# A planned three-layer kernel on one core: the order of the work found anew with other prices for changes of array form, and 49 filler products where there were 60

## The chip, the cores and the metric

The kernel runs on one core of one Trainium2 chip. The metric is the device time of one execution in microseconds (us). Lower is better. TensorE is called PE here, VectorE DVE, ScalarE ACT, GpSimd POOL, and SyncE, which issues the DMAs, SP.

## What is computed

Three layers follow each other on 4 batches of 576 positions, all in float32: an attention of 8 heads over a window of 64 positions, a gated layer that mixes positions, and a top-2 choice among 4 experts, each of which is a causal attention of one head.

```python
# 1: windowed attention, head_dim 64
scores = scale * q @ k^T ; mask = (rel >= 0) & (rel < 64)
x = softmax(where(mask, scores, -1e9)) @ v          # to (B, S, 512)
# 2: gated mixing of positions
h = maximum(x @ w_in, 0) ; u, v = h[..., :512], h[..., 512:]
v_n = (v - mean(v)) / sqrt(var(v) + 1e-6)
v_s = einsum('ts,bsd->btd', w_spatial, v_n) + b_spatial
x = (u * v_s) @ w_out
# 3: top 2 of 4 experts
logits = x @ w_gate ; topk = argpartition(-logits, 2)[..., :2] ; w = softmax(selected logits)
for e in range(4):
    a = softmax(causal(scale * (x @ wq[e]) @ (x @ wk[e])^T))
    out += where(e in topk, w, 0) * (a @ (x @ wv[e]) @ wo[e])
```

## The kernel before, in words

The large products take each float32 operand as a high and a low part and add three products (`mm3`); these are the instructions that stand in the trace as `xh,w`, `xl,w`, `w,xh` and so on. They use the whole array, 128 rows by 128 columns. Other products use parts of it, and their groups stand in the trace with the array in front of the shape:

- form 0: the whole array (`b_v`, `b_u`, `b_mix`, `fold` in the first stage, `c_qk`, `c_v`, `c_vt`, `c_wo` in the second), and the transposes (`p_t`, L647; `tr`, L1329), which have no form of their own before
- form 1: scores of the windowed attention, `s_mm`, 64*64, 24 instructions for one *couple* (two groups of three blocks of 64 queries)
- form 2: products of probabilities and values, `pv` and `c_pv`, 128*64
- form 3: scores of the experts' attention, `three`, 64*128

The order of the instructions on every engine is made by a planner that runs while the kernel is built (class `Planner`, L169 to L306). Each piece of work is a node (`N(...)`) with a price in ns on each engine that may do it, what it depends on, the buffers that it takes, and a priority out of the list `KEY`. The planner keeps a clock. When an engine is free, it takes the ready node with the lowest key whose buffers are free. `SWITCH` is added to the key of a node on PE that would change the array's form, `DRAIN` is the time that it counts for such a change. Where DVE, ACT or POOL may do a node, `DVE_BIAS`, `POOL_BIAS` and `EFT` decide how willingly an engine takes it. What it puts out is a fixed order on each engine with semaphore waits; on the chip nothing is chosen.

There are two planned stages, one after the other. Stage 1 holds 1,130 nodes: loads, preparation of the weights (`prep64` and others, on DVE, ACT and POOL), the windowed attention of all batches (24 couples: `s_mm`, masked scores L629, exponentials L635, normalisation L643, transposes, copies, `pv`), the gated layer of all batches, and the `fold` of `w_out` into the experts' weights. The gated layer of one batch runs beside the windowed attention of the next. Stage 2 is the experts' layer, in which P is normalised at L1317 on DVE or POOL and then transposed. A node of stage 2 comes behind all of stage 1 on its engine.

`heat` makes filler products on the identity matrix: `WARM` = 8 of them in front of everything, and `FILL` = 60 nodes that have the highest key there is, so that the planner takes one where nothing else is ready on PE. All of them must be placed before stage 1 ends. Each is two instructions in the trace (`bank<-ident`).

Of the kernel before, what the change touches and what calls it, by code (L numbers as in the profile page):

```python
# [26 lines left out]
SWITCH = (51316.5562883, 56444.76665)  # L27
A_BIAS = 10098.0
C_BIAS = 162315.0
DVE_BIAS = (924.812225719, 2809.18155958)  # L30
POOL_BIAS = (605.73769693, 3223.06614942)
WARM = 8
FILL = 60
LOADS = (-130000, -120000, -43801, -5807, 14591, 18276, 34028)
EFT = (348.130120865, 591.3127716)
# [6 lines left out]
    1e+09, 1e+09, 1e+09, 1e+09, 1e+09, 1e+09, 1e+09, 1e+09, 1e+09, 1e+09, 1e+09, 1e+09, 1e+09, -433949.337, -310768.212, -410360.675, -53326.873, -46012.043, -29718.587, 29893.476, 36423.798, 130640.442, 48760.892, -102410.634,  # L42
# [132 lines left out]
class Node:  # L175
    __slots__ = ("on", "emit", "prio", "wait", "next", "ready", "alloc", "use", "end", "by", "late", "form", "nth", "sbuf")


class Planner:

    LAT = 200.0, 165.0, 130.0, 75.0, 900.0
    ISSUE, WAY, RATE, FLIGHT = 475.0, 650.0, 360.0, 8

    DRAIN = (0.0, 145.0, 145.0, 92.0), (0.0, -78.0, 0.0, 0.0), (0.0, 0.0, -78.0, 0.0), (0.0, 0.0, 0.0, -92.0)

    CLASH, BEHIND = 1.0, 2200.0

    def __init__(self):
        self.nodes, self.free, self.prio = [], [1500.0, 2000.0, 2900.0, 7600.0, 560.0], 0.0
        self.moved, self.unit = [-1e9] * self.FLIGHT, 0
        self.phase = self.form = self.asked = 0
        self.sbuf = False

    def node(self, on, emit, deps=(), alloc=(), use=(), prio=None, late=None, form=0, sbuf=False):
        n = Node()
        n.form, n.nth, n.sbuf = form, self.asked, sbuf
# [1317 lines left out]
```

## Time and profile before

| | us |
|---|---|
| median of 3 runs | 441.62 |
| the runs | 441.45 to 443.12 |
| the profiled execution | 441.42 |
| its span, first to last instruction | 439.6 |
| PE busy in it | 432.1 |
| DVE, ACT, POOL busy | 288.6, 275.8, 90.0 |

The profile is of one execution. A timeline row is an instruction or a run of like ones: its start, how long it lasts, engine, line, operation, what it writes and reads, the array in use and the shape. Products overlap, so the length of a row holds the end of the pipe too, and the distance between two starts is what a block costs in a row of others. A line can be that of a helper: L416 is `mm`, through which all products go, L440 is `sub`.

### The profile page before, as it was taken

To read this page: it belongs to the slowest core of one execution; us is meant where nothing else is said; L and a number is where in the kernel's file an instruction comes from. 1 tells how busy PE (TensorE), PEld (TensorE's weight loads), DVE (VectorE), ACT (ScalarE), POOL (GpSimd) and SP (SyncE) were. 2 spreads that over 40 slices of the span, in tenths; PEclk is the share of its full clock that TensorE was granted. 3 is DMA by queue.
4 is the path that set the end of the run, shared out by engine and by line. 5 is a ranking of instruction groups with operands and counts; after the bars stand their busy time and mean duration, and the time that the engine had idled before them with its cause. 6 is when DMAs were issued, how large, how long until landed. Compare 5 with 4: busy or idle time off the path is not lost.

```text
span 439.6 us, 10921 instructions
## 1 busy us (share of the span) xinstructions
PE 432.1 (98%) x4058; PEld 390.0 (89%) x4058; DVE 288.6 (66%) x1238; ACT 275.8 (63%) x883; POOL 90.0 (20%) x132
## 2 busy tenths in 40 slices
PE   8999999999999999999999999999999999999997
PEld 7988989998889989998999999999799978987775
DVE  4999998695787583354435444977654956498750
ACT  4899986787785273352433352867576748557873
POOL 4556754121041050001100120120012101110000
PEclk9999999999999999999999999999999999999999
DMA  8995614364145020121001000000020002000114
GB/s 269 339 343 151 238 51 154 96 205 120 38 108 147 1 73 0 49 73 49 1 1 50 0 1 1 0 2 2 1 97 1 1 1 98 1 0 2 49 51 143
DMA packets 31079, 33.11 MB, mean 75 GB/s; under 512 B 1905, under 2 KB 24689, under 8 KB 31026
## 3 DMA queue, kind: packets, MB, share of 16 engines
q1 hardware_dynamic: 31026, 32.41, 23.5%
q8 instruction: 32, 0.52, 0.5%
q14 instruction: 21, 0.17, 0.1%
HBM read 27.68 MB, written 4.72 MB: 74 GB/s over the span
## 4 chain that ended last, share of the span: by engine, by line
PE 84%; DVE 10%; ACT 3%; issue 1%; DMA 1%; POOL 1%; SPq 0%; DVEq 0%; POOLq 0%; ACTq 0%
PE bank L416 75%; PE bank L1329 5%; PE bank L647 4%; DVE p L1307 3%; DVE p L1300 2%; DVE p L1317 1%; ACT p L1313 1%; DMA kt<-in_kT_dram 1%; POOL p L1317 1%; DVE mc L1315 1%; DVE qk L440 0%; DVE mc L1316 0%; ACT pa L635 0%; DVE t2w L440 0%; DVE pa L629 0%
## 5 line engine op out<-in xcount | busy, mean ns | idle before, releaser
L416 PE MATMUL bank<-xh,w 128*128 128x288 f32 x512 | 109.5, 298 | 0.0
L416 PEld LDWEIGHTS bank<-xh,w 128*128 128x128 f32 x512 | 84.1, 188 | 1.4 <-issue 0.3
L416 PE MATMUL bank<-xl,w 128*128 128x288 f32 x256 | 75.5, 295 | 0.0
L416 PE MATMUL bank<-w,xh 128*128 128x512 f32 (+1 forms) x256 | 64.8, 343 | 0.0
L635 ACT ACTIVATE pa<-pa,mx 128x128 f32<-128x128 f32 x144 | 55.8, 393 | 12.7 <-DVE mx L629 12.6
L1313 ACT ACTIVATE p<-p,mc 128x256 f32<-128x256 f32 (+4 forms) x72 | 41.5, 577 | 15.5 <-DVE mc L1307 13.7
L416 PEld LDWEIGHTS bank<-xl,w 128*128 128x128 f32 x256 | 48.1, 188 | 0.4
L416 PEld LDWEIGHTS bank<-w,xh 128*128 128x128 f32 x256 | 43.0, 188 | 5.0 <-DVE mx L651 0.2
L416 PE MATMUL bank<-w,xl 128*128 128x512 f32 (+1 forms) x128 | 43.2, 338 | 0.0
L1317 POOL TENSOR_SCALAR p<-p,mc,fx 128x384 f32<-128x384 f32 (+4 forms) x22 | 14.6, 664 | 133.8 <-DVE mc L1316 66.8
L416 PE MATMUL bank<-wsp_h,vh 128*128 128x288 f32 x128 | 38.9, 304 | 0.0
L416 PE MATMUL bank<-wsp_l,vh 128*128 128x288 f32 x128 | 37.7, 294 | 0.0
L416 PE MATMUL bank<-wsp_h,vl 128*128 128x288 f32 x128 | 37.7, 294 | 0.0
L1307 DVE CUSTOM_DVE_ANT_0 p<-bank,cmask 128x512 f32<-128x512 f32 (+3 forms) x64 | 28.8, 487 | 4.8 <-PE bank L416 2.4
L629 DVE CUSTOM_DVE_ANT_0 pa<-bank,mask 128x128 f32<-128x128 f32 x120 | 28.2, 286 | 4.4 <-PE bank L416 4.3
L853 POOL TENSOR_TENSOR st<-st,nhalf 128x1 f32<-128x1 f32 (+1 forms) x20 | 11.8, 592 | 92.2 <-DVE st L852 56.6
L427 ACT ACTIVATE pg<-bank 128x512 f32<-128x512 f32 (+4 forms) x80 | 29.7, 438 | 0.7 <-PE bank L1329 0.2
L1329 PE MATMUL bank<-ident,p 128*128 128x128 f32 x192 | 27.2, 276 | 1.7 <-DVE p L1317 0.7
L427 ACT ACTIVATE pt<-bank 128x384 f32<-128x384 f32 x41 | 18.4, 486 | 15.8 <-PE bank L647 15.8
L635 ACT ACTIVATION_READ_ACCUMULATOR pa<-pa,mx 128x1 f32 x144 | 27.6, 192 | 0.0
L416 PEld LDWEIGHTS bank<-w,xl 128*128 128x128 f32 x128 | 24.1, 188 | 2.8
L1329 PEld LDWEIGHTS bank<-ident,p 128*128 128x128 f32 x192 | 21.6, 140 | 5.5 <-DVE p L1317 2.6
(193 smaller groups left out, 989.9 us busy)
## 6 DMA issues: line engine op xcount, KB each, us to landing
vt<-in_v_dram SPq DMA_DIRECT2D x12, 512.0 KB, 5.0
qa<-in_qT_dram SPq DMA_DIRECT2D x44, 96.0 KB, 4.4
out_dram<-ot SPq DMA_DIRECT2D x15, 256.0 KB, 2.1
y<-in_w_in_dram SPq DMA_DIRECT2D x7, 512.0 KB, 6.2
kt<-in_kT_dram SPq DMA_DIRECT2D x12, 288.0 KB, 5.3
y<-in_w_outT_dram SPq DMA_DIRECT2D x4, 512.0 KB, 4.2
y<-in_wspT_dram SPq DMA_DIRECT2D x2, 576.0 KB, 4.0
vt<-in_kq_dram SPq DMA_DIRECT2D x2, 384.0 KB, 3.8
```

What stands on the lines that cost most here:

```text
L416: pe.matmul(o, lhsT, rhs, start=start, stop=stop)
L427: act.activation(o, i, AF.Copy)
L629: dve.tensor_tensor_reduce(out=pa[:, j, :], in0=ps[:, j * 128:(j + 1) * 128], in1=mask(j), scale=-0.125, scalar=3.0e38, op0=ALU.add, op1=A ...
L635: act.activation(pa[:, j, :], pa[:, j, :], AF.Exp, bias=mx[:, j, 0:1], scale=-1.0, accum_out=mx[:, j, 1:2])
L647: pe.transpose(ps2[:, j * 128:(j + 1) * 128], pa[:, j, :], ident)
L853: a = N((POOL, 464), lambda e: pool.tensor_tensor(out=st[:m, 9:10], in0=st[:m, 8:9], in1=nhalf[:m], op=ALU.pow), [n1], use=[st])
L1300: dve.tensor_tensor_reduce(out=P[HALF[y], a0:a1], in0=ps[y][HALF[y], :HS], in1=cmask[HALF[y], 0:HS] if i == 0 else tmask[HALF[y]], scale=- ...
L1307: tops = [N((DVE, t_tt(L)), lambda _, ps=ps: dve.tensor_tensor_reduce(out=P[:, cs], in0=ps[:, cs], in1=cmask[:, 512 - L:512], scale=-0.125 ...
L1313: a = N((ACT, 284 + 0.87 * L), lambda e: act.activation(P[:, cs], P[:, cs], AF.Exp, bias=mc[:, 0:1], scale=-1.0, accum_out=mc[:, 2:3]), to ...
L1315: a = N((DVE, 70), lambda e: dve.tensor_scalar(mc[:, 3:4], mc[:, 2:3], 1e-9, None, op0=ALU.add), [a], use=[mc], prio=prio)
L1317: a = N({POOL: 328 + 0.832 * L, DVE: 90 + 0.52 * L}, lambda e: engs[e].tensor_scalar(P[:, cs], P[:, cs], mc[:, 3:4], fx[:, I, ev:ev + 1], ...
L1329: pe.transpose(ps[:, j * m:(j + 1) * m], P[:, c0 + j * 128:c0 + (j + 1) * 128], ident)
```

## The change

All of it is in the planner's input and in its prices. `KEY`, with one number for each node, is another list (2,028 numbers that are not a filler's, and 49 fillers'). The fillers go from 60 to 49. `SWITCH`, which was added once where PE goes between form 0 and any other, is now multiplied by the time of the change, out of a table for every pair of forms, and transposes are a form of their own (4), which costs nothing beside form 0. The prices of nodes on PE no longer hold the changes. The normalisation of P at L1317 is priced at 190 ns and not 90 on DVE, besides its elements. The biases of DVE and POOL change. No instruction's shape, operand or buffer changes.

```diff
-SWITCH = (51316.5562883, 56444.76665)
+SWITCH = (3449.06880151, 1241.9455123)
-DVE_BIAS = (924.812225719, 2809.18155958)
-POOL_BIAS = (605.73769693, 3223.06614942)
+DVE_BIAS = (909.043169196, 5820.53335932)
+POOL_BIAS = (256.434349454, 4103.69459824)
-FILL = 60
+FILL = 49
-EFT = (348.130120865, 591.3127716)
+EFT = (137.341113842, 3173.43987937)
 KEY = (
...
-    DRAIN = (0.0, 145.0, 145.0, 92.0), (0.0, -78.0, 0.0, 0.0), (0.0, 0.0, -78.0, 0.0), (0.0, 0.0, 0.0, -92.0)
+    DRAIN = ((0.0, 138.0, 137.0, 191.0, 0.0),
+             (212.0, 0.0, 158.0, 212.0, 165.0),
+             (204.0, 151.0, 0.0, 204.0, 157.0),
+             (194.0, 141.0, 140.0, 0.0, 147.0),
+             (0.0, 145.0, 144.0, 198.0, 0.0))
...
-                    key = n.prio + (SWITCH[self.phase] if e == PE and (n.form > 0) != (self.form > 0) else 0.0), n.nth
+                    key = n.prio + (SWITCH[self.phase] * self.DRAIN[self.form][n.form] if e == PE else 0.0), n.nth
...
-        S_N[n0] = S_N[n0 + 1] = top = N((PE, 816), s_mm, kn + [Q_N[n0], Q_N[n0 + 1], S_N.get(n0 - 1)], alloc=bank, use=hk, prio=prio,
+        S_N[n0] = S_N[n0 + 1] = top = N((PE, 654), s_mm, kn + [Q_N[n0], Q_N[n0 + 1], S_N.get(n0 - 1)], alloc=bank, use=hk, prio=prio,
...
-            a = N((PE, 327), p_t, [a], alloc=[ps2, pt], use=[pa], prio=prio)
+            a = N((PE, 327), p_t, [a], alloc=[ps2, pt], use=[pa], prio=prio, form=4)
...
-        o = N((PE, 848), pv, done + [PV_N.get(k[:2]) for k in grp] + vn, alloc=[ps3] + new, use=pts + hv, prio=prio,
+        o = N((PE, 699), pv, done + [PV_N.get(k[:2]) for k in grp] + vn, alloc=[ps3] + new, use=pts + hv, prio=prio,
...
-        a = N({POOL: 328 + 0.832 * L, DVE: 90 + 0.52 * L}, lambda e: engs[e].tensor_scalar(
+        a = N({POOL: 328 + 0.832 * L, DVE: 190 + 0.52 * L}, lambda e: engs[e].tensor_scalar(
```

The same is done in stage 2: `three`, `c_pv` and `c_wo` lose what their prices held for a change, and the transposes `tr` get form 4.

## Rows read from the trace of the kernel before

**Rows 1.** Page: busy us by engine; PE's granted clock, 40 slices, tenths.

```profile
PE 432.1 (98%) x4058; PEld 390.0 (89%) x4058; DVE 288.6 (66%) x1238; ACT 275.8 (63%) x883; POOL 90.0 (20%) x132
PEclk9999999999999999999999999999999999999999
```

**Rows 2.** By stage: length, engines' busy us, granted clock, DMA share, GB/s.

```profile
0.00:25.30 25.30, 23.83 (x298) 21.81 (x299) 19.39 (x98) 17.61 (x66) 13.36 (x36) 1.00 0.96 306
25.30:60.00 34.70, 33.70 (x354) 29.12 (x353) 32.09 (x136) 33.80 (x115) 21.58 (x23) 1.00 0.65 215
60.00:256.00 196.00, 196.00 (x1962) 182.72 (x1961) 120.13 (x463) 107.14 (x357) 36.66 (x49) 1.00 0.23 66
258.60:436.30 177.70, 175.98 (x1429) 153.76 (x1427) 115.32 (x544) 114.48 (x339) 18.15 (x25) 1.00 0.07 26
```

**Rows 3.** Timeline, PE, 0 to 30 us: start, us, engine, line, operation, tiles, shape.

```profile
5.18 1.56 PE L416 MATMUL bank<-vt 64*64 64x128 f32 x24
8.65 0.89 PE L416 MATMUL bank<-vt 64*64 64x128 f32 x24
24.39 0.83 PE L416 MATMUL bank<-ident 128*128 128x128 f32 x6
25.31 0.71 PE L416 MATMUL bank<-w,xh 128*128 128x512 f32 x2
```

**Rows 4.** Timeline of DVE, 8 to 34 us.

```profile
23.12 0.56 DVE L643 TENSOR_TENSOR pa<-pa,mx 128x384 f32<-128x384 f32 x1
24.54 0.33 DVE L440 TENSOR_TENSOR xl<-bank,xh 128x192 fp32r<-128x192 f32 x1
```

**Rows 5.** Timeline of PE, 60 to 80 us.

```profile
63.04 0.29 PE L416 MATMUL bank<-xh,w 128*128 128x288 f32 x1
63.26 0.92 PE L416 MATMUL bank<-pt,vt 128*64 128x64 f32 x24
64.11 0.89 PE L416 MATMUL bank<-kt,qa 64*64 64x128 f32 x24
...
65.78 0.89 PE L416 MATMUL bank<-kt,qa 64*64 64x128 f32 x24
66.59 0.40 PE L416 MATMUL bank<-wsp_h,vh 128*128 128x288 f32 x1
66.83 0.30 PE L416 MATMUL bank<-wsp_l,vh 128*128 128x288 f32 x1
...
78.18 1.62 PE L416 MATMUL bank<-pt,vt 128*64 128x64 f32 x48
79.73 0.40 PE L416 MATMUL bank<-wsp_h,vh 128*128 128x288 f32 x1
```

**Rows 6.** Timeline of PE, 255 to 262 us.

```profile
256.02 2.84 PE L416 MATMUL bank<-ident 128*128 128x128 f32 x24
258.62 0.49 PE L416 MATMUL bank<-w,xh 128*128 128x260 f32 x2
```

**Rows 7.** Timeline of POOL, 248 to 266 us.

```profile
254.13 0.81 POOL L440 TENSOR_TENSOR xl<-pa,xh 128x288 fp32r<-128x288 f32 x1 [9.05 <-ACT xh L427]
```

**Rows 8.** Waits of PE's weight loads from 256 us: us, times, longest.

```profile
PEld bank L1329 <- DVE p L1317: 2.6, 7, 0.7
PEld bank L1329 <- POOL p L1317: 1.5, 4, 0.6
```

**Rows 9.** Groups by line and shape: busy us, mean ns, idle before them.

```profile
L1317 DVE TENSOR_SCALAR p<-p,mc,fx 128x384 f32<-128x384 f32 x8 | 3.8, 479 | 0.1
L1317 POOL TENSOR_SCALAR p<-p,mc,fx 128x384 f32<-128x384 f32 x8 | 6.2, 770 | 37.8 <-DVE mc L1316 22.4 <-ACT oh L427 15.4
```

**Rows 10.** Page: groups of masked scores, exponentials and copies of stage 1.

```profile
L629 DVE CUSTOM_DVE_ANT_0 pa<-bank,mask 128x128 f32<-128x128 f32 x120 | 28.2, 286 | 4.4 <-PE bank L416 4.3
L635 ACT ACTIVATE pa<-pa,mx 128x128 f32<-128x128 f32 x144 | 55.8, 393 | 12.7 <-DVE mx L629 12.6
L427 ACT ACTIVATE pt<-bank 128x384 f32<-128x384 f32 x41 | 18.4, 486 | 15.8 <-PE bank L647 15.8
```

More of the change, by code (lines that the diff above doesn't have):

```diff
@@ L41 @@
     1e+09, 1e+09, 1e+09, 1e+09, 1e+09, 1e+09, 1e+09, 1e+09, 1e+09, 1e+09, 1e+09, 1e+09, 1e+09, 1e+09, 1e+09, 1e+09, 1e+09, 1e+09, 1e+09, 1e+09, 1e+09, 1e+09, 1e+09, 1e+09,
-    1e+09, 1e+09, 1e+09, 1e+09, 1e+09, 1e+09, 1e+09, 1e+09, 1e+09, 1e+09, 1e+09, 1e+09, 1e+09, -433949.337, -310768.212, -410360.675, -53326.873, -46012.043, -29718.587, 29893.476, 36423.798, 130640.442, 48760.892, -102410.634,
[85 rows of a table removed]
+    1e+09, 1e+09, -367151.352, -349921.894, -357607.274, -121393.737, -140326.89, -100931.392, -99031.673, -73271.671, -58056.097, -50110.204, -166770.302, -122982.601, -358667.696, -358903.944, -385197.421, -358202.174, -359433.768, -163314.009, -121448.521, -110265.225, -229129.906, -275481.363,
[84 rows of a table added]
 )
@@ L1253, in scores @@
                 ps = [r_sc.new(), r_sc.new()]
-                a = N((PE, 92 + 3 * t_mm(HS)), lambda _, ps=ps, i=i: three(
+                a = N((PE, 3 * t_mm(HS)), lambda _, ps=ps, i=i: three(
                     [p[:, :HS] for p in ps], (S - 64, S - 128), i * HS, (i + 1) * HS),
@@ L1269, in go @@
                 c += w
-        a = N((PE, 92 + sum(3 * t_mm(128 * I + 128) for I in tiles)), go, deps, alloc=ps + pp + gets, use=[qk], prio=prio, form=3)
+        a = N((PE, sum(3 * t_mm(128 * I + 128) for I in tiles)), go, deps, alloc=ps + pp + gets, use=[qk], prio=prio, form=3)
         started(a)
@@ L1336, in unit @@
         f, an = a, PG_N[key][:1]
-        a = N((PE, nj * 109), tr, [f] + an, alloc=[ps], use=[P], prio=prio)
+        a = N((PE, nj * 109), tr, [f] + an, alloc=[ps], use=[P], prio=prio, form=4)
         a = N(on_copy(nj * m, 1), tc_, [a], use=[ps, pg], prio=prio)
@@ L1344, in unit @@
             a = N((PE, 109), lambda _: pe.transpose(pt[:64, :128], P[:, 512:576], ident), [f] + PG_N[key][:1], alloc=[pt],
-                  use=[P], prio=prio)
+                  use=[P], prio=prio, form=4)
             a = N(on_copy(128), lambda e_: copy(e_, pg[HALF[hb], 3, :, 64 * hb:64 * hb + 64],
@@ L1372, in c_pv @@
         cs = slice(i0, i0 + 256)
-        o = N((PE, 800 if grp == 0 else 2200), go, PG_N[b, pr, grp] + V2_N[b] + (VT_N[b] if grp else []) + ([] if new else O_N[b, pr][:1]),
+        o = N((PE, 651 if grp == 0 else 2056), go, PG_N[b, pr, grp] + V2_N[b] + (VT_N[b] if grp else []) + ([] if new else O_N[b, pr][:1]),
               alloc=[ps] + new, use=[pg, v2] + ([vt] if grp else []), prio=prio, form=2)
@@ L1417, in c_wo @@
             return
-        a = N((PE, 78 + 6 * t_mm(512)), lambda e: mm3(ps.t, [
+        a = N((PE, 6 * t_mm(512)), lambda e: mm3(ps.t, [
             ((part(0, pr), part(1, pr)), (view(wh.t)[:, pr, :], view(wl.t)[:, pr, :])) for pr in range(2)]),
```

169 rows, old and new, of the table KEY are left out of this document.

## The prediction, made before the change was run

> **What bounds the kernel now.** I read the page's busy times first. TensorE (PE) is busy for 98% of the span at a granted clock of full speed in every slice [rows 1], so time can only go where PE does something that the result does not need, or stands. The table by stage says where that is [rows 2]: from 25.3 us on, PE is busy in practically all of every stage, while VectorE (DVE) and ScalarE (ACT) have slack from 60 us on (DVE 120 of 196 us). Busy is not the same as useful, so the third view is PE's timeline, read by the distance from one start to the next. It shows four things.
>
> The head. Until 25.31 us PE waits for its first 128x512 products, and the 60 filler products stand in the gaps: 48 of them there, each a pair of instructions on `ident` (fp32 goes as two), the last three at 24.39 us [rows 3]. What ends the head is the attention chain and not PE: DVE's last `xl` at 24.54 us comes 0.4 us ahead of that first product [rows 4].
>
> The changes of array form. A block of 24 `pv` products (array 128*64) takes 0.85 us to the next start where a block of another form follows it, and two of them in a row take 1.55 us (78.18 to 79.73) [rows 5]: 0.70 for the one that is followed by its like, so the change costs 0.15. A visit from 128x288 products and back, at 63.26 to 66.59 us, has 0.22 us instead of 0.13 in front of its first product, and 0.24 instead of 0.13 behind its first full product [rows 5]. In between lie four blocks, `pv`, `s_mm`, `pv`, `s_mm`, with 0.85, 1.67 (for two) and 0.81 us, 3.33 in all, against 2.70 without changes (0.70 for a `pv`, and 0.65 for an `s_mm`, an estimate: 0.81 less about the same loss, since the trace never has two `s_mm` in a row). The visit pays 0.09 + 0.63 + 0.11 = 0.83 us for five changes: 0.17 us each. Going through PE's timeline I count 51 such changes between 25 us and 224 us and 36 from 273 us to the end, so 87 x 0.17 = 14.8 us of the span. Transposes beside full products show no such loss, and they are not counted.
>
> The end of stage 1. The other 12 fillers stand together from 256.02 to 258.62 us [rows 6]. What the first product of stage 2 reads (`xh`, `xl` of batch 3) was finished by 254.94 us, at the end of GpSimd's (POOL's) last subtraction [rows 7]. These 2.60 us cover nothing.
>
> The waits. In stage 2 PE's weight loads of transposes wait 4.1 us in all for the normalised P (2.6 on DVE, 1.5 on POOL) [rows 8].
>
> **The change part by part.** The arithmetic stays. Two things happen to the program: 11 products on `ident` go, and all other instructions are put in another order, on engines chosen anew where a choice exists. The remaining lines are prices for the planner that makes this order.
>
> *Fillers.* The head took 48 in the old order. Its gaps come from loads and from DVE, which keep their work, so I take 48 again and one left over at the end of stage 1. The saving is 11 x 2 x 0.108 us (2.60 us over 24 instructions [rows 6]) = 2.4 us. Bounds: 2.6 us at most (all 12 gone), zero if the new order's stage 1 ends in a wait for its last subtraction. What is late next is `c_vt`, which reads `zt`, made on ACT and DVE at the start of stage 2: PE arriving 2.4 us sooner must take tiles of `c_v` first, and three of them need no `zt`.
>
> *Changes of form.* Before, the planner added 51,317 to a candidate's key in stage 1 where PE would go between the full form and any other, and nothing between `s_mm` and `pv`. Now it adds 3,449 per nanosecond of the change's price: 476,000 for full to `s_mm`, 545,000 for `s_mm` to `pv`, 731,000 for `s_mm` to full. The keys of stage 1 in the diff (all but the first 1,119 are stage 2's) lie between -477,000 and 129,000, those of `s_mm` between -435,000 and -139,000. So in stage 1 nearly no key can outweigh a change: PE stays in its form until nothing of that form (or, from the full form, no transpose) is ready. Sequences like `pv`, `s_mm`, `pv`, `s_mm` [rows 5] should become `pv`, `pv`, `s_mm`, `s_mm`. If all 18 couples behind the head went in pairs, about half of the 51 changes would go: 25 x 0.17 = 4.3 us; none is the other end. Pairs need two couples' `pt` at once, for which the ring has just four tiles, so I take a quarter to a third of them, 14: 2.4 us. In stage 2 the price is 1,242 per nanosecond, 171,000 to 263,000, against keys that reach over 2.3 million: about the old proportion (56,445 against 548,000). There I take 2 of 36 changes, 0.3 us, with bounds of zero and a third (2.0 us). But holding a form makes something else late: couples start later. I charge 0.3 us for that, so this part is worth 2.4 us.
>
> The trace prices a change at 0.17 us. The Trainium skill, "TensorE: Matmul & The Clock Gate", section "Part 2: What happens when you issue a matmul", puts the time for the last column to leave the array at about 128 cycles. At 2.4 GHz that is an estimate of 53 ns, by which 16 fewer changes would be worth 0.9 us and not 2.7. The rows above show three times as much, and I stay with the rows.
>
> *Prices for the normalisation of P.* DVE's price in stage 2 rises by 100 ns; a 128x384 one takes 479 ns on DVE and 770 on POOL [rows 9]. The old formula gave 290 ns, the new one gives 390. Nothing on the chip changes but who does it: 50 were on DVE and 22 on POOL. A row moved to POOL takes 0.48 us off DVE and makes its own chain 0.29 us longer. All waits for these rows together are 4.1 us [rows 8]; a third of that either way (1.4 us) is the bound, and I take zero, since DVE is busy for only 115 of 178 us there [rows 2].
>
> *The rest of the new order.* SP's loads, POOL's and DVE's work in the head all have new keys, and POOL's bias falls from 606 to 256 ns in stage 1. DVE is busy for 19.4 of the first 25.3 us [rows 2], from 10 us on without a pause, and its weight preparation for the first product lies in the same queue as the softmax of the first couples. One step put wrongly ahead of the last `xl`, such as a normalisation of 0.56 us [rows 4], delays everything behind it. Bounds: three such steps, 1.7 us, either way; taken as zero.
>
> The sum against the profiled execution: 441.42 us, which is a span of 439.6 and 1.8 around it, and lies 0.2 under the median of 441.62. 441.4 - 2.4 - 2.4 = **436.6 us**.
>
> **The rivals.**
>
> *A. Only the fillers.* Forms are held, but the waits that this makes eat the 2.4 us. For it: DVE and ACT are close behind PE until 60 us (32.1 and 33.8 of 34.7 us [rows 2]), and a couple needs them between `s_mm` and `pv`. Against: from 60 us they have slack. Time: 441.4 - 2.4 = 439.0 us.
>
> *B. The stretch at the end of stage 1 becomes a wait.* The changed order ends stage 1 with its last `mix` and splits instead of with folds, so that what the fillers stood in becomes idle time and the other gains are given back too. In the old order the last subtraction, 0.81 us on POOL, ended 1.1 us ahead of PE's last fold [rows 6, 7]; a `mix` that comes a fold later uses that up. Time: 441 us, no change.
>
> *C. Slower: PE starves at the batch boundary.* This speaks against the new rule itself. If PE stays with full products until none is ready, the next batch's attention begins when there is nothing left to cover it. The first couple's chain then lies open: 0.82 us of `s_mm`, three masked scores of 0.29, three exponentials of 0.39 [rows 10], a normalisation of 0.56 [rows 4], three transposes (0.33 by the kernel's own price) and a copy of 0.49 [rows 10], some 4.2 us. Behind it DVE sets the pace: per couple 6 x 0.29 and 2 x 0.56, and with `xl` and the small steps some 3.5 us, against 2.3 us of PE (0.82 + 0.85 + 0.65). That is 1.2 us for each of the other five couples of the batch, 6 us. Time with one batch of three exposed: 441.4 - 4.8 + 10 = 446.6 us. It decides when the last full products of a batch run out before its successor's first two couples are through. Against it: in the old order PE was busy in all of 60 to 256 us [rows 2], and the planner sees such a gap in its own clock.
>
> In the trace the granted clock is full throughout, and still the first `s_mm` block, early in the head, took 1.56 us against 0.89 later [rows 1, 3]. The Trainium skill, "TensorE: Matmul & The Clock Gate", section "Why this matters for your kernels", warns that an idle PE is put back to half its clock. By that rule case C with idle stretches would be dearer: two blocks at the slow pace of the head add 1.3 us, about 448 us. No stretch of this trace shows the clock falling; I give it 0.03 of C's chance.
>
> *D. Much better.* Half the changes of both stages and the head's 1.7 us gone, 441.4 - 2.4 - 7.4 - 1.7: under 432 us.
>
> **How the numbers follow.** Forecast (432 to 439 us, most likely 436.6): 0.55. A: 0.15, split about evenly over the edge of half a per cent, which is 439.2 us. B: 0.10. C: 0.15. D: 0.05. Half a per cent, 2.2 us, is about what a measurement of this kernel can tell from no change. Faster by more: 0.55 + 0.08 + 0.05 = 0.68. Within: 0.07 + 0.10 = 0.17. Slower: 0.15. The range is 432.0 to 442.0 us: the low end is the forecast with the upper bounds of fillers and of changes in stage 1 (2.1 us) and most of the head's and of stage 2's, the high end is B with 1 us of wait on top; C and D, 0.20 together, lie outside.
>
> **What would show it.** Right: at the end of stage 1 one or two fillers instead of 12; 48 in the head; blocks of 48 `pv` or `s_mm` in PE's timeline and some 35 to 40 changes between the head and 224 us; PE without idle rows from 60 us to the start of stage 2; the first 128x512 product at 25 +- 1 us. Wrong: a head that is longer by more than 1 us; waits of transposes or of `pv` for `pa` and `pt` in the middle of stage 1 (C); as many changes as before (A); an idle row at the end of stage 1 (B); POOL rows of L1317 that PE waits for by more than 4.1 us in all.

## The result, and the profile after

The changed kernel takes **437.27 us** (median; 436.44 to 437.52), the kernel before 442.25 us on the same chip (441.45 to 443.12): a ratio of 0.988, 95% interval 0.986 to 0.991. The profiled execution took 437.31 us with a span of 435.2. So the time fell by 5.0 us by the medians and by 4.1 us between the two profiled executions; 436.6 us were predicted, a fall of 4.8. The time was right. Where it came from was not, as the profile shows first and the experiments then take apart.

The page, busy us by engine:

```profile
PE 428.8 (99%) x4036; PEld 386.0 (89%) x4036; DVE 270.6 (62%) x1185; ACT 276.9 (64%) x894; POOL 127.3 (29%) x176
```

By stage, with the columns of [rows 2]:

```profile
0.00:23.90 23.90, 22.43 (x284) 20.23 (x284) 17.37 (x85) 16.51 (x59) 12.78 (x36) 1.00 0.96 311
23.90:60.00 36.10, 35.78 (x371) 30.93 (x372) 33.52 (x133) 35.35 (x126) 25.61 (x28) 1.00 0.64 203
60.00:256.00 196.00, 195.42 (x1955) 181.55 (x1954) 106.10 (x437) 110.14 (x365) 57.76 (x72) 1.00 0.23 68
256.50:431.90 175.40, 174.62 (x1429) 152.81 (x1427) 113.64 (x531) 114.48 (x345) 30.62 (x42) 1.00 0.08 26
```

Against [rows 1], PE is busy for 3.3 us less, and POOL for 37 us more, 21 of them from 60 to 256 us and 12 in stage 2. From 60 to 256 us PE was never idle before; now it is for 0.6 us.

PE's timeline (start, length, engine, line, operation, tiles, array, shape): the first 128x512 product, four blocks of one visit to the attention, the end of stage 1, stage 2's first `c_vt`, its first scores, and the last product:

```profile
23.89 0.70 PE L419 MATMUL bank<-w,xh 128*128 128x512 f32 x2
...
63.56 0.89 PE L419 MATMUL bank<-kt,qa 64*64 64x128 f32 x24
64.38 0.92 PE L419 MATMUL bank<-pt,vt 128*64 128x64 f32 x24
65.22 0.89 PE L419 MATMUL bank<-kt,qa 64*64 64x128 f32 x24
66.04 0.92 PE L419 MATMUL bank<-pt,vt 128*64 128x64 f32 x24
66.89 0.55 PE L650 MATMUL bank<-ident,pa 128*128 128x128 f32 x3
...
256.38 0.38 PE L419 MATMUL bank<-ident 128*128 128x128 f32 x2
...
259.61 1.61 PE L419 MATMUL bank<-w,zt 128*128 128x260 f32 x12
...
271.83 2.27 PE L419 MATMUL bank<-qk 64*128 64x288 f32 x24
...
431.65 0.28 PE L419 MATMUL bank<-w,ol 128*128 128x256 f32 x1
```

In the kernel before, the first scores and the last product stood here (timeline of PE):

```profile
273.93 2.29 PE L416 MATMUL bank<-qk 64*128 64x512 f32 x24
...
436.04 0.28 PE L416 MATMUL bank<-w,ol 128*128 128x256 f32 x1
```

Three readings. First, a single filler is left at the end of stage 1 (256.38, two instructions) where [rows 6] had 12. The other 48 are placed by 33 us, six of them now behind the first 128x512 product, which comes 1.4 us sooner than in [rows 3]. Second, `s_mm`, `pv`, `s_mm`, `pv` still alternate, 3.33 us for the four (63.56 to 66.89), as in [rows 5]. Counted through the timeline, 52 changes of form lie between the first 128x512 product and the first scores in both kernels, and 36 behind where there were 35. (The prediction's 51 and 36 are the same 87 changes of before, with the one into the first scores counted behind. As there, transposes count with the whole array, and so do the 16 `w,xt` products that the trace shows on 128*64: these stand 0.23 to 0.24 us from start to start like their 128x512 neighbours on the whole array.) Third, half the gain lies behind the first scores: up to them it is 2.1 us (273.93 to 271.83), and from them to the last product **2.3 us** (162.11 to 159.82), where the prediction had 0.3.

The same can be split by kind. From the first product to the last PE takes 4.4 us less. Taking off each distance from one start to the next what its kind takes undisturbed, and the kernel's own new table for each change of form, leaves the waits. By this sum fillers give 2.4 us, changes of form 0.5 us, and waits 1.5 us: 2.1 less in stage 2, 0.6 more before it. Behind the first scores it needs no table of undisturbed times: both kernels run the same 1,306 products there, in 2.3 us less, of which 0.15 are changes of form.

The waits of PE's weight loads from 256 us on, and the groups of P's normalisation from there:

```profile
PEld bank L1332 <- POOL p L1320: 1.2, 2, 0.9
PEld bank L1332 <- DVE p L1320: 0.2, 1, 0.2
```

```profile
L1320 DVE TENSOR_SCALAR p<-p,mc,fx 128x384 f32<-128x384 f32 (+4 forms) x41 | 20.4, 498 | 0.6
L1320 POOL TENSOR_SCALAR p<-p,mc,fx 128x128 f32<-128x128 f32 (+4 forms) x31 | 19.7, 638 | 116.5 <-PE bank L419 27.3 <-ACT p L1316 25.0 <-DVE mc L1319 19.3
```

The 4.1 us of [rows 8] are 1.4 us now. PE's own waits for the same rows (1.1 us before, 0.6 after) lie inside these, so 4.1 and 1.4 are the times; the 5.2 and 2.0 in some of the expectations below add both and count those stretches twice. POOL does 31 of the 72 normalisations and did 22.

### The profile page after: what moved, and what is told of

Its sections match the earlier page's. It is cut to its first block, busy times and chain, and to the rows that moved or that the text cites. A ratio compares the mean times of both kernels' runs of the same rounds, so it can differ in the third digit from the quotient of the medians.

```text
span 435.2 us, 10930 instructions
## 1 busy us (share of the span) xinstructions
PE 428.8 (99%) x4036; PEld 386.0 (89%) x4036; DVE 270.6 (62%) x1185; ACT 276.9 (64%) x894; POOL 127.3 (29%) x176
## 4 chain that ended last, share of the span: by engine, by line
PE 84%; ACT 8%; DVE 5%; issue 1%; DMA 1%; POOL 0%; SPq 0%; ACTq 0%; POOLq 0%; DVEq 0%
PE bank L419 76%; PE bank L1332 5%; PE bank L650 3%; ACT pa L638 3%; DMA y<-in_wspT_dram 1%; ACT pa L644 1%; DVE p L1310 1%; DVE xl L443 1%; ACT bank L765 1%; ACT xh L430 1%; ACT pt L430 1%; DVE p L1303 1%; ACT ut L438 0%; ACT wsp_h L430 0%; DVE bank L772 0%
## 5 line engine op out<-in xcount | busy, mean ns | idle before, releaser
L419 PE MATMUL bank<-xh,w 128*128 128x288 f32 x512 | 111.3, 300 | 0.6 <-ACT pt L430 0.6
L1316 ACT ACTIVATE p<-p,mc 128x384 f32<-128x384 f32 (+4 forms) x72 | 41.6, 579 | 20.2 <-DVE mc L1310 19.1
L1320 POOL TENSOR_SCALAR p<-p,mc,fx 128x128 f32<-128x128 f32 (+4 forms) x31 | 19.7, 638 | 116.5 <-PE bank L419 27.3
L430 ACT ACTIVATE pg<-bank 128x512 f32<-128x512 f32 (+4 forms) x80 | 30.6, 441 | 1.5 <-PE bank L1332 1.0
L921 DVE TENSOR_TENSOR y<-bank,ut 128x288 f32<-128x288 f32 x24 | 10.9, 455 | 25.8 <-PE bank L419 25.6
L646 POOL TENSOR_TENSOR pa<-pa,mx 128x384 f32<-128x384 f32 x13 | 11.7, 899 | 49.9 <-ACT pa L638 24.1
```

What stands on the lines that cost most here:

```text
L419: pe.matmul(o, lhsT, rhs, start=start, stop=stop)
L430: act.activation(o, i, AF.Copy)
L646: engs[e].tensor_tensor(out=pa.t, in0=pa.t, in1=mx[:, :, 3:4].to_broadcast([128, 3, 128]), op=ALU.mult)
L921: dve.tensor_tensor(out=o, in0=ps[:, :HS], in1=u[:, d, tk], op=ALU.mult)
L1316: a = N((ACT, 284 + 0.87 * L), lambda e: act.activation(P[:, cs], P[:, cs], AF.Exp, bias=mc[:, 0:1], scale=-1.0, accum_out=mc[:, 2:3]), to ...
L1320: a = N({POOL: 328 + 0.832 * L, DVE: 190 + 0.52 * L}, lambda e: engs[e].tensor_scalar(P[:, cs], P[:, cs], mc[:, 3:4], fx[:, I, ev:ev + 1], ...
```

## The experiments

To move single steps, the planner's choice was replaced in most of these kernels by a list of what it had chosen: `ORDER`, with the number of a node, its engine (0 PE, 1 ACT, 2 DVE, 3 POOL, 4 SP) and the planner's time. The rest of the kernel stays, and only the lines shown differ. The body of `mm` is then L536, `copy` L547, `sub` L560 (one more in kernels with 60 fillers).

```diff
+        for nth, e, t in ORDER[self.phase]:
+            self.start(left.pop(nth), e, t, lambda m: None)
```

Heads differ from run to run: in the seven profiles with the old order of stage 1 the same block of 48 `pv` ([rows 5], 78.18) starts between 77.89 and 79.75 us, with nothing edited before it. The three with 60 fillers lie at 77.89 to 78.18, the four with 49 at 78.89 to 79.75; whether the fillers at the far end of the stage have a part in that is not shown (in the new order the one profile with 60, 78.43, lies among the others). So besides the ratio each run is read between marks of PE's timeline behind the head: that block of 48 `pv` (or the first 128x512 product), the first scores, the last product. Between the last two of these marks the five profiles with the old order of stage 2 lie between 162.02 and 162.13 us, the six with the new one between 159.77 and 159.83.

**The fillers alone** (`e_bef49`).

```diff
-FILL = 60
+FILL = 49
-       (50, 0, 254268), (51, 0, 254496), (52, 0, 254724), ... (60, 0, 256548),
```

> The old order on every engine, written out as a list, with the 11 last filler products of stage 1 left out and nothing else. Theory 1 (the fillers at the end of stage 1 cover nothing): 2.4 us less than before, about 0.9946 of its time, PE's first product of stage 2 at 256.2 us instead of 258.6. Rival (they stand where PE would wait for the splits and for zt): no change, with an idle row of PE between 256 and 259 us.

Measured 441.04 us, 0.9983 (0.9967 to 0.9999): 0.8 us, not 2.4. PE's timeline:

```profile
79.22 1.62 PE L536 MATMUL bank<-pt,vt 128*64 128x64 f32 x48
...
257.06 0.38 PE L536 MATMUL bank<-ident 128*128 128x128 f32 x2
...
259.32 0.51 PE L536 MATMUL bank<-w,zt 128*128 128x260 f32 x2 [0.46 <-ACT zt L547]
260.23 1.46 PE L536 MATMUL bank<-w,zt 128*128 128x260 f32 x10 [0.40 <-POOL zt L560]
...
273.88 2.29 PE L536 MATMUL bank<-qk 64*128 64x512 f32 x24
```

From the `pv` block to the first scores it is 194.66 us, 1.1 less than before (78.18 to 273.93, 195.75). The missing 1.3 us stand in the timeline: the old order brings `c_vt` after one tile of `c_v`, and its two halves wait for `zt`, once for ACT's copies and once for POOL's subtraction. With 12 fillers in front, the same 12 products ran as one unbroken row:

```profile
260.13 1.61 PE L416 MATMUL bank<-w,zt 128*128 128x260 f32 x12
```

So the fillers did cover something: half of their own length, in the old order.

**The same, with `c_vt` two tiles later** (`e_zt`, and once more as `e_zt2`).

```diff
-       (1156, 2, 257384), (1157, 0, 258222), (1123, 1, 258422), ...   # 1157 is c_vt
+       (1156, 2, 257384), (1123, 1, 258422), ... (1133, 0, 261116), (1157, 0, 261116),
```

> The old order with the last 11 filler products of stage 1 left out, and the product c_vt, which reads zt, moved behind two more tiles of c_v on PE (its copies and sums on the other engines move with it; nothing else is edited). Theory: the run without the fillers gained 0.8 us where the fillers take 2.4 us, because PE then stood still for zt (0.46 and 0.40 us before the two zt products, 0.7 and 0.6 us before their weight loads, among them); with two tiles of c_v ahead of it zt is there in time, and the gain is the fillers' own time: 2.4 us, a ratio of 0.9945, with no row of PE waiting for zt above 0.2 us. Rival: what ends last there is not zt but the work behind it (the first scores of stage 2 and their exponentials), and the wait moves to the next product: the same 0.998 as without the move.

> The kernel e_zt again. In its first run the stretch from 88 us to the end was 2.45 us shorter than in the kernel before, as forecast, and the first 88 us, in which nothing was edited, were 1.2 us longer, so the time fell by 0.9 us alone. Theory (the head differs from run to run and the gain is real): the stretch from 88 us is again 2.4 us shorter, and the time falls by 1.5 us or more, 0.9965 or lower. Rival (the longer head belongs to this kernel): 0.998 again, with the profile's first 88 us a microsecond longer again.

Measured 440.53 us, 0.9977 (0.9960 to 0.9993), and the second time 439.85 us, 0.9960 (0.9942 to 0.9977). PE's timeline of the first and of the second:

```profile
79.34 1.62 PE L536 MATMUL bank<-pt,vt 128*64 128x64 f32 x48
...
261.72 1.61 PE L536 MATMUL bank<-w,zt 128*128 128x260 f32 x12
...
272.62 2.29 PE L536 MATMUL bank<-qk 64*128 64x512 f32 x24
```

```profile
78.89 1.62 PE L536 MATMUL bank<-pt,vt 128*64 128x64 f32 x48
...
272.17 2.29 PE L536 MATMUL bank<-qk 64*128 64x512 f32 x24
```

`c_vt` runs in one row again, and in both profiles the stretch from the `pv` block to the first scores is 193.28 us: 2.47 us less than before, the 11 fillers' own 2.4. What was between the marks behaved as forecast, twice. The medians show less of it, 0.9 and 1.8 us; these profiles reached the `pv` block 1.2 and 0.7 us later than the kernel before did, with the same instructions up to there, and took 0.3 and 0.6 us longer from the last product to the end of the span (3.56 us before). The theory of `e_zt` held between the marks and missed its ratio; that of `e_zt2` held by both, if barely. Why the head should be late in both is not settled: the seven profiles spread over 1.9 us there.

**The fillers put back into the new order** (`e_aft60`, with the changed kernel itself beside it, `e_after`).

```diff
-FILL = 49
+FILL = 60
+       (50, 0, 257363), (51, 0, 257591), ... (60, 0, 259643),
```

> The new order with 11 filler products put back at the end of stage 1, at the place of the one that is left there: 60 in all, nothing else edited. Theory: in the new order zt is not read until two tiles later, so nothing late lies behind the fillers and they cost their own time, 11 x 2 x 0.108 us = 2.4 us: 0.9884 of the kernel before becomes 0.994. Rival: the engines ahead of stage 2 run late in the new order as in the old, and the fillers cover a wait as they did there, so they cost 0.8 us or less: 0.990.

> The changed kernel as it is, run beside the others on one chip so that the runs with the new order have their own base. All theories: 0.988 to 0.989 of the kernel before, 437 us.

Measured 439.33 us, 0.9946 (0.9929 to 0.9963), beside 436.42 us, 0.9884 (0.9863 to 0.9904). PE's timeline with 60 and with 49:

```profile
23.89 0.70 PE L537 MATMUL bank<-w,xh 128*128 128x512 f32 x2
...
274.09 2.27 PE L537 MATMUL bank<-qk 64*128 64x288 f32 x24
```

```profile
23.39 0.70 PE L419 MATMUL bank<-w,xh 128*128 128x512 f32 x2
...
271.20 2.27 PE L419 MATMUL bank<-qk 64*128 64x288 f32 x24
```

250.20 against 247.81 us: 2.39 us, which is the fillers' own time (22 x 0.108 us), as the theory had it; by the medians it is 2.9 us. In the new order nothing late lies behind them. The same fillers were worth 1.1 us between marks in the old order and 2.4 in the new one.

**One stage of each order** (`e_b1a2`: the old stage 1 with one filler at its end, the new stage 2; `e_a1b2`: the new stage 1, the old stage 2).

```diff
-ORDER = (stage 1 before, stage 2 before)
+ORDER = (stage 1 before, stage 2 after)      # e_b1a2
+ORDER = (stage 1 after, stage 2 before)      # e_a1b2
```

> Stage 1 in the old order with 49 fillers, stage 2 in the new order. Theory 1 (4.4 us = 2.4 fillers + 2.2 fewer waits in stage 2 + 0.5 form changes - 0.7 more waits in stage 1): 2.4 + 2.2 + 0.2 = 4.8 us less than before, 0.989 of its time. Rival (what the new order gives, it gives by its changes of form in stage 1): 2.4 us less, 0.9946.

> Stage 1 in the new order (49 fillers), stage 2 in the old order. Theory 1: the fillers' 2.4 us, and stage 1 otherwise level (0.3 us fewer changes, 0.5 to 0.7 us more waits): 2.0 to 2.4 us less than before, 0.995 of its time. Rival (form changes of stage 1): 4 us less or more, 0.991 or below.

Measured 437.33 us, 0.9905 (0.9884 to 0.9926), and 439.94 us, 0.9966 (0.9949 to 0.9983). PE's timeline of `e_b1a2`, then of `e_a1b2`:

```profile
261.71 1.46 PE L536 MATMUL bank<-w,zt 128*128 128x260 f32 x10 [0.48 <-DVE zt L560]
...
273.78 2.27 PE L536 MATMUL bank<-qk 64*128 64x288 f32 x24
...
433.61 0.28 PE L536 MATMUL bank<-w,ol 128*128 128x256 f32 x1
```

```profile
24.15 0.70 PE L536 MATMUL bank<-w,xh 128*128 128x512 f32 x2
...
258.60 0.51 PE L536 MATMUL bank<-w,zt 128*128 128x260 f32 x2 [0.47 <-ACT zt L547]
259.50 1.47 PE L536 MATMUL bank<-w,zt 128*128 128x260 f32 x10 [0.40 <-POOL zt L560]
...
273.14 2.29 PE L536 MATMUL bank<-qk 64*128 64x512 f32 x24
...
435.16 0.28 PE L536 MATMUL bank<-w,ol 128*128 128x256 f32 x1
```

Against the kernel before, that is 4.5 and 1.9 us less where the theories had 4.8 and 2.0 to 2.4; the forecast ratios lie inside both intervals, and those of the rival, changes of form in stage 1, outside. Against `e_bef49`, the new stage 2 is worth 3.7 us by the medians and 2.9 between marks, and the new stage 1 1.1 us. The first is the larger part by far, and the stretch behind the first scores carries 2.3 us of it: 159.83 us, against 162.10 in `e_bef49`. The waits for `zt` take both stages to go: `c_vt` third, as the new stage 2 has it, still waits 0.48 us behind the old stage 1, for DVE's part of `zt`:

```profile
259.19 2.47 DVE L560 TENSOR_TENSOR zt<-y,zt 128x128 fp32r<-128x128 f32 x1
```

It ran beside two subtractions of POOL (2.81 us from 258.29) and took 2.47 us. In the changed kernel POOL's two began 1.2 us sooner, counted from the `pv` block, and DVE's took 1.33 us beside them; in the kernel before it took 0.29 us with POOL idle. The new stage 1 followed by the old stage 2 waits for it as `e_bef49` did. Of the 1.1 us of the new stage 1 the two profiles show 0.8, and 0.3 of that is in changes of form, by the table. The first 128x512 product does come sooner with it (22.89 to 24.20 us in seven profiles, 24.44 to 25.71 in the seven with the old stage 1), but the six fillers that it leaves behind that mark are 1.3 us, so that this is no gain.

**One price alone** (`e_bef190`).

```diff
-        a = N({POOL: 328 + 0.832 * L, DVE: 90 + 0.52 * L}, lambda e: engs[e].tensor_scalar(
+        a = N({POOL: 328 + 0.832 * L, DVE: 190 + 0.52 * L}, lambda e: engs[e].tensor_scalar(
```

> The kernel before with its own keys and its 60 fillers, and one figure changed: the planner's price of the normalisation of P on DVE, 90 + 0.52 a column, becomes 190 + 0.52 a column, as in the new version. The order is planned anew with it. Theory (the price alone): the planner sees DVE as later than it did and hands POOL more of the 72 normalisations; PE's waits for normalised P in stage 2 fall from 5.2 us to near the 2.0 us of the new version, and the time falls by 2 us or more: 0.995 or lower. Rival (the search of the keys, not the price): the old keys were found for the old price, the order falls apart elsewhere by as much as it gains, and the time is the same or longer: 1.00 or above.

Measured 442.34 us, 1.0025 (1.0006 to 1.0044): the rival. PE's timeline, and the larger of the waits of its weight loads for P, from 258 us:

```profile
273.74 2.29 PE L416 MATMUL bank<-qk 64*128 64x512 f32 x24
...
436.59 0.28 PE L416 MATMUL bank<-w,ol 128*128 128x256 f32 x1
```

```profile
PEld bank L1329 <- POOL p L1317: 2.2, 5, 0.7
```

The price does what it is for: POOL takes 29 normalisations, and the waits of PE's weight loads for them fall from 4.1 to 2.4 us. But with the old keys the end of stage 2 falls apart by more. PE's order is the old one up to 396 us, and up to there the stretch is 0.3 us shorter; behind it 1.1 us are lost, with 41 changes of form behind the first scores where there were 35, and a wait of 1.0 us for ACT's copy into `pg`, the longest of which was 0.2 us. The whole stretch takes 162.85 us, 0.7 more than before. So the gain of stage 2 belongs to the new order as a whole, not to this figure. The way round, the old price with the new keys, leaves the planner without an order and wasn't tried; nor were other prices.

**What the waits for P are worth** (`e_short_b` in the old order, `e_short_a` in the new one).

```diff
-            P[:, cs], P[:, cs], mc[:, 3:4], fx[:, I, ev:ev + 1], op0=ALU.mult, op1=ALU.mult), [a, fn],
+            P[:, c0:c0 + 64], P[:, c0:c0 + 64], mc[:, 3:4], fx[:, I, ev:ev + 1], op0=ALU.mult, op1=ALU.mult), [a, fn],
```

> The old order with its 60 fillers; the normalisation of P (one instruction for each of the 72 tiles) works on the first 64 columns of the tile alone, where it worked on all 128 to 576. Left out: the rest of P's columns stay as the exponential left them, so what is computed behind them differs. No instruction is added, taken out or moved. Read from the first score product of stage 2 (273.9 us) to the end, which the head of the kernel doesn't touch: 162.4 us in the old order, 160.1 us in every run with the new order of stage 2. Theory (PE's waits for normalised P are the difference of the two orders): the normalisation is over 0.2 to 0.35 us sooner each time, the waits of PE and its weight loads for it (5.2 us) nearly vanish, and the stretch comes to 160 us or less. Rival (the orders differ in something else): it stays above 161.5 us.

> The same cut in the new order with its 49 fillers: the normalisation of P works on the first 64 columns of each tile alone, the rest of P stays as the exponential left it. Theory: the new order has 2.0 us of such waits, so the stretch from the first score product to the end falls by less than in the old order, from 160.1 to 159 us or a little above, and the two orders end within 0.7 us of each other there. Rival (the orders differ in something else): the new order keeps its 2.3 us in that stretch.

One profile each. PE's timeline, old order and new order:

```profile
273.64 2.29 PE L537 MATMUL bank<-qk 64*128 64x512 f32 x24
...
433.28 0.28 PE L537 MATMUL bank<-w,ol 128*128 128x256 f32 x1
```

```profile
272.41 2.27 PE L536 MATMUL bank<-qk 64*128 64x288 f32 x24
...
430.60 0.28 PE L536 MATMUL bank<-w,ol 128*128 128x256 f32 x1
```

The old order comes to 159.64 us, 2.5 less, and the waits for the normalised P come to 0.6 us: as expected, the old order with those waits gone is as good as the new one. But the new order gains too, 1.6 us, to 158.19, and the two stay 1.45 us apart where less than 0.7 was expected. So the theory holds by half. The normalisation's length explains 0.85 us of the 2.3 between the two orders; both have then about the same waits for it (0.6 and 0.5 us). The shorter normalisation takes some 14 us of work off DVE and POOL together, so more than these waits may have moved with it. Of the other 1.45 us, some 0.7 lie between one transpose and the next (the sum over all distances from start to start, above 0.109 us each, is 1.2 us in the old and 0.5 us in the new one) and 0.15 in changes of form. The rest, 0.6 us, is spread over many rows and stays open.

**Pairs by hand** (`e_pair`, and once more as `e_pair2`). In the new order, eight `s_mm` blocks or `pv` blocks of stage 1 were moved in PE's order alone, each to stand beside its like. One of them:

```diff
-       (100, 3, 37481), ... (108, 3, 38069), (312, 0, 38071), ... (440, 4, 38746), (388, 0, 38890), (313, 1, 39238),
+       (100, 3, 37481), ... (108, 3, 38069), (388, 0, 38071), (312, 0, 38071), ... (440, 4, 38746), (313, 1, 39238),
```

> The changed kernel's order with eight blocks of stage 1 moved on PE alone, so that score products of two couples stand next to each other and their value products too; 51 changes of form by the program instead of 64. If a change costs 0.17 us on PE: 13 x 0.17 = 2.2 us less than the changed kernel, about 435.0 us or 0.984 of before. If it is hidden, or if the couples' softmax comes later by it: no change against the changed kernel (0.9884 of before) or 1 us more.

> The kernel e_pair again, on another chip: the new order with eight blocks of stage 1 moved on PE alone, so that two products of one form stand together. Theory: 13 changes of form fewer at 0.17 us are 2.2 us, of which the first run showed 1.5 us against the changed kernel by the medians; 0.985 of the kernel before, 435 us. Rival (the first run was lucky in its head): 0.988, like the changed kernel.

Measured 435.76 us, 0.9865 (0.9843 to 0.9887), and 435.81 us, 0.9876 (0.9858 to 0.9893). PE's timeline of the first, then of the second:

```profile
22.89 0.70 PE L536 MATMUL bank<-w,xh 128*128 128x512 f32 x2
...
61.95 1.54 PE L536 MATMUL bank<-kt,qa 64*64 64x128 f32 x48
63.42 1.62 PE L536 MATMUL bank<-pt,vt 128*64 128x64 f32 x48
64.97 0.55 PE L767 MATMUL bank<-ident,pa 128*128 128x128 f32 x3
...
269.59 2.27 PE L536 MATMUL bank<-qk 64*128 64x288 f32 x24
```

```profile
23.79 0.70 PE L536 MATMUL bank<-w,xh 128*128 128x512 f32 x2
...
270.71 2.27 PE L536 MATMUL bank<-qk 64*128 64x288 f32 x24
```

Here are the pairs that the prediction expected of the planner: `s_mm` x48 in 1.47 us and `pv` x48 in 1.55, 3.02 us for the four blocks that took 3.33 in the changed kernel. Two changes fewer save 0.31 us, 0.155 each. In all there are 39 changes between the first 128x512 product and the first scores, 13 fewer; at 0.155 that is 2.0 us. The stretch between these marks fell by 1.1 and 0.9 us (246.70 and 246.92 against 247.81), so, by subtraction, about half was given back in waits. The expected 2.2 us did not come: the forecast ratios, 0.984 and 0.985, lie just outside the intervals, and 0.988, like the changed kernel, lies inside both. By the medians the kernel is 0.6 us better than `e_after` and 1.5 better than the changed kernel in its first runs. It has the lowest medians of all that ran, and no more can be said.

## Why the prediction was right in its time and wrong in its steps

**Fillers: the right size, for a reason that was wrong.** The count (48 early, one left) and the price (2.4 us) held in the new order, by `e_aft60`. The step "These 2.60 us cover nothing" failed: it looked at `xh` and `xl`, which the first product reads, and not at `zt`, which the 13th reads. The prediction did name `zt` as what is late next, and that PE "must take tiles of `c_v` first"; it did not see that the old order takes a single one, that in 2.4 us less `zt` would not be there, and that POOL makes a part of it too (the 0.40 us in `e_bef49`). In the old order the fillers were worth 1.1 us between marks. The new order made them worth 2.4, with `c_vt` third and POOL's work at the end of stage 1 sooner; `e_b1a2` and `e_a1b2` show that either alone does not do it.

**Changes of form: 2.7 us were forecast, 0.5 came.** This is the step that failed outright. The count went from 52 to 52 in stage 1, not to 35 or 40; other pairs of forms were chosen (8.4 us by the new table before, 8.1 after), and stage 2 gave 0.15 us in place of 0.3. The price was right: 0.17 us against 0.155 measured by `e_pair`, and `s_mm` 0.65 us behind its like, as estimated. The 53 ns worked out from the Trainium skill ("TensorE: Matmul & The Clock Gate", "Part 2: What happens when you issue a matmul") are a third of what was measured. What failed is "nearly no key can outweigh a change: PE stays in its form until nothing of that form (or, from the full form, no transpose) is ready". The weight was read correctly; readiness was not. Each `s_mm` depends on the one before it (`S_N.get(n0 - 1)` in the diff), a `pv` on the one before it where the two share a pair of heads (`PV_N`), and in the planner's clock a node is ready only `LAT` behind what it depends on, 0.2 us for PE. So at the moment when an `s_mm` ends, the next is never ready, a `pv` can be, and the heavy key has nothing to hold on to. That is read from the code. The timelines fit it: in both kernels no two of the 24 `s_mm` blocks stand together, and each has four pairs of `pv`, all of couples that share no pair of heads, while 12 of the 23 couples that follow one another do share one. Orders planned without that latency could not be had, so as the cause it is argued and not shown; what `e_pair` shows is that PE runs two `s_mm` one right behind the other and loses nothing.

**Normalisation of P and the new order of stage 2: taken as zero, 2.3 us.** The prediction gave +-1.4 us to a term that it priced as a move of rows from DVE to POOL. The stretch behind the first scores fell by 2.3 us in every run with the new stage 2. The price by itself, with the old keys, cost 0.7 us there (`e_bef190`), so the gain belongs to the new order, partly in the waits for P (4.1 to 1.4 us by the rows, about 0.85 us of the difference by `e_short_b` and `e_short_a`). What the rest of it is stays open in part. The sign that was there to read was the 4.1 us of [rows 8]: with PE the bound, a new order that serves PE better can take from such rows; two thirds of them went, and a bound of one third was too narrow.

**Head: taken as zero, and about zero.** The first 128x512 product is 1.3 us sooner (23.7 against 25.0 us, means of seven profiles each), just outside the 25 +- 1 us in the changed kernel's profile (23.89), and gives that back in the fillers behind it. Later couples were charged with 0.3 us of waits; all of the waits ahead of stage 2 grew by 0.6.

**The rivals.** A (only the fillers, 439.0 us) is about what the new stage 1 did by itself (439.94 us, `e_a1b2`). It fell by stage 2. B's mechanism, a wait at the end of stage 1, is real: it stands in `e_bef49` at 259 us, 1.3 us long, behind another product than the one B named; the new order avoids it. C did not happen: PE is idle for 0.6 us of the 196 us from 60 us on. The granted clock is full in all 40 slices, so the dearer form of C had no occasion.

That the sum came out is luck, for two errors met: 2.2 us too much for the forms, 2.1 us missed in stage 2's waits. With 0.3 us more waits before it than were charged, 4.8 becomes the 4.4 us that the profiles show between PE's first and last product.

## What to carry to other kernels

Before calling a filler or a gap useless, follow every operand that the next dozen instructions read, not the next one's alone: a stretch that covers nothing for the first product can cover half its length for the thirteenth. A penalty in a scheduler acts only on candidates that it regards as ready at that moment; look at its latencies and dependencies before counting on its weights. Where the head differs by a microsecond from run to run, compare kernels between marks behind it that hold the same work: eleven profiles, in two groups, agreed within 0.1 us in each, which medians of a dozen runs didn't.

## What the runs showed of the hardware

The start-up is the largest source of spread seen here: the same instructions reached the same block between 77.89 and 79.75 us, while the 160 us behind the first scores repeated within 0.1 us (159.77 to 159.83 in six profiles). The end spread by 0.7 us (3.5 to 4.2 us from the last product to the end of the span in 14 profiles). And a change between `s_mm` and `pv` costs 0.155 us each way on average, with PE at its full granted clock and the next operands there.
